# Reordering the first loads and casts of a fused dynamic convolution and squared-ReLU feed-forward kernel

## The chip, the cores and the metric

The kernel runs on one core of one Trainium2 chip. The metric is device time in microseconds (us). The profile is one execution taken by the hardware profiler. With one core busy there is no second die to compare, so the granted TensorE clock of each run (its mean as a share of full speed) is used beside its time where it matters. In this kernel TensorE does the matmuls, VectorE the softmax and the bands, ScalarE exponentials and copies, and GpSimd memsets, casts and the issue of those loads that cast on the way (casting loads).

## The reference

```python
# dynamic convolution: 7 taps per token and head, softmax over the taps
w = exp(weight_gen - max); w = w / (sum(w) + 1e-9)           # (8, 4096, 8, 7)
out = einsum('bshk,bskhg->bshg', w, x_unf)                    # x: (8, 4096, 192), causal, zero padded
# feed-forward on the 32768 tokens
h = maximum(out @ w_in, 0.0)                                  # w_in: (192, 2048)
result = (h * h) @ w_out                                      # w_out: (2048, 192), result float32
```

## The kernel before

A block is 512 tokens; there are 64. For each, softmax rows become a banded matrix ("bands", `bd`, on VectorE), small matmuls apply it to x (the convolution, `yp`), ScalarE copies the result out (`y`), and two products with w_in (`h`) and w_out (`o`) follow. Softmax weights go to DRAM (`vd`) and come back as rows (`wr`). The first block takes its rows straight from the first softmax tile (`v_first`) by small moves within the on-chip memory (row moves). The startup, cut:

```python
def cast_w_in(q, straight, crossed):
    ...
    straight(out=w_i[:, 0, c], in_=w_sa[q])
    crossed(out=w_i[RT:P, 1, c], in_=w_sa[q][0:RT])
    crossed(out=w_i[0:RT, 1, c], in_=w_sa[q][RT:P])
    straight(out=w_i[:, 2, c], in_=w_sb[q])        # last 64 rows of w_in, loaded twice
...
spin(38)                        # 38 matmuls on zeros ("warming matmuls")
band_mask()
nc.gpsimd.memset(v_first[2], 0.0)
nc.gpsimd.memset(v_big, 0.0)
...
s0.load(nc.sync)
s1.load(nc.sync)
x_load_f32(0)
load_w_in(0)
load_w_in(1)
s0.exp(0, s0.rh)
s1.exp(0, s1.rh)
x_cast(0, act)
s0.recip(0, s0.rh)
s0.scale(0, s0.rh, nc.vector)
s1.recip(0, s1.rh)
wr_load_sbuf(s0, (0, 2, 1, 3, 4), (nc.scalar, nc.gpsimd))
s0.store(nc.scalar)
cast_w_in(0, act, pool)
wr_load(1)
x_load_f32(1)
load_w_out(0)
for i in (0, 2, 1, 3, 4):
    st_band(0, (i,))
st_conv_alloc(0)
st_conv(0)
spin(4)
st_y_evac(0)
s1.scale(0, s1.rh, nc.vector)
s1.store(nc.sync)
cast_w_in(1, pool, pool)
x_cast(1, pool)
wr_load(2)
x_load(2)
load_w_out(1)
for q in range(WQ):
    cast_w_out(q, pool)
s2.load(nc.sync)
st_bands(1, 0)
st_bands(1, 1)
... # then the loop over blocks j: products of j, convolution of j+1, bands of j+2, x_load(j+3)
```

The softmax here doesn't subtract the row's maximum and nothing guards it: scores larger than these inputs give would overflow.

## Time and profile before

| | before |
|---|---|
| median of three runs | 794.05 us (792.2 to 794.29) |
| span of the profiled run | 791.0 us |
| first real product starts | 23.01 us |
| convolution of block 2 starts | 32.84 us |
| TensorE busy, 80 to 140 us | 59.96 of 60 us |

The views used are the page (busy lines, slices), the chain that ended last in order of time (start, length, what; short lines of issue and queue are left out unmarked), the timeline (start, length, engine, source line, operation, output<-input, count, and in brackets the idle time before and what ended it) and the table by stretch. The prediction shows the lines but one, the convolution of block 2 in the timeline:

```profile
32.84 0.98 PE L339 MATMUL yp<-bd,xt 128*32 128x104 f16 x72
```

### The profile page before, as it was taken

To read this page: it belongs to the slowest core of one execution; us is meant where nothing else is said; L and a number is where in the kernel's file an instruction comes from. 1 tells how busy PE (TensorE), PEld (TensorE's weight loads), DVE (VectorE), ACT (ScalarE), POOL (GpSimd) and SP (SyncE) were. 2 spreads that over 40 slices of the span, in tenths; PEclk is the share of its full clock that TensorE was granted. 3 is DMA by queue.
4 is the path that set the end of the run, shared out by engine and by line. 5 is a ranking of instruction groups with operands and counts; after the bars stand their busy time and mean duration, and the time that the engine had idled before them with its cause. 6 is when DMAs were issued, how large, how long until landed. Compare 5 with 4: busy or idle time off the path is not lost.

```text
span 791.0 us, 32666 instructions
## 1 busy us (share of the span) xinstructions
PE 773.3 (98%) x14890; PEld 679.7 (86%) x14890; DVE 586.7 (74%) x1040; ACT 605.4 (77%) x756; POOL 81.8 (10%) x98
## 2 busy tenths in 40 slices
PE   5998999999999999999999999999999999999998
PEld 2787888888888888888988888888888888888887
DVE  5888777777877768777778777877778777666653
ACT  3676877877877877877877877887787787787785
POOL 7501000010001000010001000011000010000000
PEclk9999999999999999999999999999999999999999
DMA  7862633435433543435433353333533334342111
GB/s 197 227 111 38 157 52 64 75 53 145 75 52 65 102 104 65 74 52 148 73 51 67 72 135 67 70 55 68 150 60 65 65 64 89 65 69 46 50 42 41
DMA packets 124009, 65.64 MB, mean 83 GB/s; under 512 B 84545, under 2 KB 121056, under 8 KB 123104
## 3 DMA queue, kind: packets, MB, share of 16 engines
q1 hardware_dynamic: 82032, 47.92, 21.6%
q0 software_dynamic: 40992, 15.28, 18.5%
q8 instruction: 116, 1.90, 1.1%
q10 hardware_dynamic: 848, 0.38, 0.2%
q14 instruction: 21, 0.17, 0.1%
HBM read 49.35 MB, written 29.36 MB: 100 GB/s over the span
## 4 chain that ended last, share of the span: by engine, by line
PE 93%; DMA 3%; DVE 2%; ACT 1%; issue 0%; SPq 0%; ACTq 0%; DVEq 0%
PE o L383 44%; PE h L364 43%; PE yp L339 6%; DMA wg<-in_weight_gen_dram 1%; DVE bd L290 1%; DMA wr<-v_first 1%; DMA x_st<-in_x_dram 1%; DMA vd<-v_first 0%; DVE g L400 0%; ACT t L394 0%; DVE v_big L194 0%; ACT ex L173 0%; DVE v_first L194 0%; DVE ssum L181 0%; DVE rcp L186 0%
## 5 line engine op out<-in xcount | busy, mean ns | idle before, releaser
L394 ACT ACTIVATE t<-h 128x1024 f16<-128x1024 f32 x512 | 482.8, 1031 | 9.4 <-PE h L364 8.8
L400 DVE TENSOR_TENSOR g<-t 128x1024 f16<-128x1024 f16 x512 | 346.9, 692 | 147.1 <-ACT t L394 146.9
L364 PE MATMUL h<-y,w_i 64*128 64x256 f16 x6144 | 362.5, 270 | 2.0 <-ACT y L352 1.2
L383 PE MATMUL o<-w_o,g 128*128 128x192 f16 x4096 | 360.0, 246 | 0.0
L383 PEld LDWEIGHTS <-g 128*128 128x128 f16 x4096 | 331.5, 98 | 26.8 <-DVE g L400 17.1
L364 PEld LDWEIGHTS <-w_i 64*128 64x128 f16 x6144 | 292.4, 94 | 51.0 <-issue 14.2
L290 DVE TENSOR_TENSOR bd<-wr,mask 128x1664 f16<-128x1664 f16 (+2 forms) x201 | 163.4, 844 | 11.2 <-DMA wr<-vd 6.2
L352 ACT CAST y<-yp 128x768 f16<-128x768 f32 x64 | 51.1, 798 | 122.8 <-PE yp L339 122.8
L251 POOL DMA_DIRECT2D xt<-in_x_dram x62 | 51.2, 826 | 460.4 <-PE yp L339 437.0
L405 ACT COPY o_sb<-o 128x384 f32<-128x384 f32 x127 | 62.9, 495 | 38.3 <-PE o L383 38.3
L339 PE MATMUL yp<-bd,xt 128*32 128x104 f16 (+13 forms) x4608 | 59.9, 203 | 10.6 <-DVE bd L290 10.5
L339 PEld LDWEIGHTS <-xt 128*32 128x32 f16 (+3 forms) x4608 | 51.2, 91 | 21.6 <-issue 21.5
L181 DVE TENSOR_REDUCE ssum<-ex 128x64 f32<-128x448 f32 (+6 forms) x49 | 25.9, 529 | 35.4 <-ACT ex L173 35.4
L194 DVE TENSOR_TENSOR v_big<-ex,rcp 128x112 f16<-128x112 f32 (+3 forms) x192 | 32.7, 234 | 1.6
L173 ACT ACTIVATE ex<-wg 128x448 f32<-128x448 f32 (+6 forms) x49 | 26.5, 541 | 5.0 <-DMA wg<-in_weight_gen_dram 4.9
L186 DVE RECIPROCAL rcp<-ssum 128x64 f32<-128x64 f32 (+6 forms) x49 | 23.3, 475 | 1.7
L245 POOL DMA_DIRECT2D xt<-in_x_dram x9 | 5.0, 552 | 85.2 <-PE yp L339 85.2
L442 PE MATMUL wp<-warm 128*128 128x512 f16 x42 | 12.4, 463 | 1.3 <-DVE warm L434 1.3
L241 POOL DMA_DIRECT2D xt<-in_x_dram x7 | 3.8, 541 | 77.5 <-PE yp L339 77.5
L442 PEld LDWEIGHTS <-warm 128*128 128x128 f16 x42 | 4.6, 114 | 7.9 <-issue 3.7
L194 DVE TENSOR_TENSOR v_first<-ex,rcp 128x112 f16<-128x112 f32 (+2 forms) x32 | 5.5, 242 | 0.2
L136 POOL CAST w_o<-wo_st 128x1536 f16<-128x1536 f32 x2 | 3.7, 1826 | 5.7 <-DMA wo_st<-in_moe_w_out_dram 5.7
(22 smaller groups left out, 25.5 us busy)
## 6 DMA issues: line engine op xcount, KB each, us to landing
out_dram<-o_sb SPq DMA_DIRECT2D x63, 384.0 KB, 2.8
xt<-in_x_dram POOLq DMA_DIRECT2D x46, 240.0 KB, 4.4
wg<-in_weight_gen_dram SPq DMA_DIRECT2D x6, 1064.0 KB, 6.0
wr<-vd SPq DMA_DIRECT2D x46, 80.0 KB, 3.0
vd<-v_big SPq DMA_DIRECT2D x7, 512.0 KB, 2.9
xt<-in_x_dram POOLq DMA_DIRECT2D x16, 192.0 KB, 3.9
wo_st<-in_moe_w_out_dram SPq DMA_DIRECT2D x2, 768.0 KB, 7.5
wr<-vd SPq DMA_DIRECT2D x17, 64.0 KB, 2.9
```

The lines of the kernel that those rows point to most:

```text
L173: nc.scalar.activation(out=self.ex[:, lo:hi].rearrange("p r g k e -> p (r g) k e"), in_=self.wg[:, lo:hi].rearrange("p r (g e) k -> p (r g ...
L181: nc.vector.tensor_reduce(out=ssum.rearrange("p r g e -> p (r g) e"), in_=self.ex[:, lo:hi].rearrange("p r g k e -> p (r g) e k"), axis=Ax ...
L194: eng.tensor_tensor(out=bass.AP(tensor=v.tensor, offset=v.offset + lo * H * SL + lo % SL * 2 + g * SL * 2, ap=[list(v.ap[0]), [H * SL + 2, ...
L251: eng.dma_start(out=dst[:, first:last], in_=ap)
L290: nc.vector.tensor_tensor(out=bd_t[j][:, H * lo : H * hi].rearrange("p (g m c) -> p g m c", g=shape[1], c=2 * SL), in0=wr_t[j][:, i : tile ...
L339: nc.tensor.matmul(out=yp_t[j][p0 : p0 + m, col + a : col + b], lhsT=x_t[j][:, i, 32 * q : 32 * q + m], rhs=bd[:, h // 2, h % 2, a - lo : ...
L352: nc.scalar.copy(out=y, in_=yp_t[j][:, 0 : NK * TH].rearrange("p (k c) -> p k c", k=NK))
L364: nc.tensor.matmul(out=h[:, half, jj, :], lhsT=w_i[r0 : r0 + RT, slot, fc * P : (fc + 1) * P], rhs=y_t[j][r0 : r0 + RT, k, :], start=(jj = ...
L383: nc.tensor.matmul(out=o[half][:, cc * Dm : (cc + 1) * Dm], lhsT=g_t[(j, fp)][:, half, jj, cc * P : (cc + 1) * P], rhs=w_o[:, fc, :], star ...
L394: nc.scalar.activation(out=t1, in_=h_t[(j, fp)], func=ActF.Relu)
L400: nc.vector.tensor_tensor(out=g, in0=t1, in1=t1, op=AluOp.mult)
L405: copy(out=o_sb_t[j][:, half], in_=o_t[j][half][:, 0 : 2 * Dm])
```

## The change

The change wants w_in on the chip and cast early, and keeps other first loads from delaying the first row moves (6.46 us before). In the loads, w_in comes right behind the first softmax input, and its last 64 rows are read once. ScalarE and VectorE take most casts of w_in from GpSimd. Block 1's rows too come straight from the softmax tile. The x rows of block 1 and w_out come by casting DMA from GpSimd, so their GpSimd casts go. Block 1's bands move ahead of softmax 1's sum and scale, and GpSimd's two memsets move back behind loads. The diff, cut; most of the removed lines are left out:

```diff
-        nc.sync.dma_start(out=w_sa[q], in_=moe_w_in[0:P, c])
-        for r0 in (0, RT):
-            nc.sync.dma_start(out=w_sb[q][r0 : r0 + RT], in_=moe_w_in[P:D, c])
+        nc.sync.dma_start(out=w_sa[q], in_=moe_w_in[0:P, c])
+        nc.sync.dma_start(out=w_sb[q], in_=moe_w_in[P:D, c])
...
+    def load_w_out(q, n):
+        nc.gpsimd.dma_start(out=w_o[:, q * NF // n : (q + 1) * NF // n], ...)   # f32 to f16
...
+        spin(36)
+        band_mask()
         s0.load(nc.sync)
-        s1.load(nc.sync)
-        x_load_f32(0)
         load_w_in(0)
         load_w_in(1)
+        x_load_f32(0)
         s0.exp(0, s0.rh)
         s0.recip(0, s0.rh)
         s0.scale(0, s0.rh, nc.vector)
+        cast_w_in(0, ...)                # four casts on ScalarE, one on GpSimd
+        wr_load_sbuf(0, s0, (0, 1, 2, 4, 3), (nc.sync, nc.gpsimd))
+        cast_w_in(1, "up", vec)
+        cast_w_in(1, "down", vec)
+        x_load(1)
+        s1.load(nc.sync)
+        for q in range(4):
+            load_w_out(q, 4)
+        nc.gpsimd.memset(v_first[2], 0.0)
+        x_cast(0, act)
+        wr_load_sbuf(1, s0, range(NT), (nc.sync,))
+        s0.store(nc.sync)
+        s2.load(nc.sync)
+        cast_w_in(1, "straight", act)
+        cast_w_in(1, "last", act)
         for i in (0, 2, 1, 3, 4):
             st_band(0, (i,))
         st_conv_alloc(0)
         st_conv(0)
         spin(4)
+        s1.exp(0, s1.rh)
         st_y_evac(0)
+        cast_w_in(1, "last up", act)
+        x_load(2)
+        nc.gpsimd.memset(v_big, 0.0)
+        st_bands(1, 0)
+        st_bands(1, 1)
+        s1.recip(0, s1.rh)
         s1.scale(0, s1.rh, nc.vector)
         s1.store(nc.sync)
         wr_load(2)
```

More of the change, by code (lines that the diff above doesn't have):

```diff
@@ L106, with cast_w_in @@
     WQ = 2
-    w_sa, w_sb, wo_st, x_st = {}, {}, {}, {}
+    NQ = Dff // WQ
+    w_sa, w_sb, x_st = {}, {}, {}
     def load_w_in(q):
-        n = Dff // WQ
-        c = slice(q * n, (q + 1) * n)
-        w_sa[q] = p_st.tile([P, n], f32, name="w_sa")
-        w_sb[q] = p_st.tile([P, n], f32, name="w_sb")
+        c = slice(q * NQ, (q + 1) * NQ)
+        w_sa[q] = p_st.tile([P, NQ], f32, name="w_sa")
+        w_sb[q] = p_st.tile([RT, NQ], f32, name="w_sb")
         nc.sync.dma_start(out=w_sa[q], in_=moe_w_in[0:P, c])
-        for r0 in (0, RT):
-            nc.sync.dma_start(out=w_sb[q][r0 : r0 + RT], in_=moe_w_in[P:D, c])
-    def cast_w_in(q, straight, crossed):
-        n = Dff // WQ
-        c = slice(q * n, (q + 1) * n)
-        straight(out=w_i[:, 0, c], in_=w_sa[q])
-        crossed(out=w_i[RT:P, 1, c], in_=w_sa[q][0:RT])
-        crossed(out=w_i[0:RT, 1, c], in_=w_sa[q][RT:P])
-        straight(out=w_i[:, 2, c], in_=w_sb[q])
-    def load_w_out(q):
-        n = NF // WQ
-        wo_st[q] = p_st.tile([P, n, Dm], f32, name="wo_st")
-        nc.sync.dma_start(
-            out=wo_st[q],
-            in_=moe_w_out[q * n * P : (q + 1) * n * P].rearrange("(c p) m -> p c m", p=P),
-        )
-    def cast_w_out(q, copy):
-        n = NF // WQ
-        copy(out=w_o[:, q * n : (q + 1) * n], in_=wo_st[q])
+        nc.sync.dma_start(out=w_sb[q], in_=moe_w_in[P:D, c])
+    def cast_w_in(q, op, copy):
+        c = slice(q * NQ, (q + 1) * NQ)
+        lower, upper = slice(0, RT), slice(RT, P)
+        out_p, slot, src = {
+            "straight": (slice(0, P), 0, w_sa[q]),
+            "up": (upper, 1, w_sa[q][lower]),
+            "down": (lower, 1, w_sa[q][upper]),
+            "last": (lower, 2, w_sb[q]),
+            "last up": (upper, 2, w_sb[q]),
+        }[op]
+        copy(out=w_i[out_p, slot, c], in_=src)
+    def load_w_out(q, n):
+        nc.gpsimd.dma_start(
+            out=w_o[:, q * NF // n : (q + 1) * NF // n],
+            in_=moe_w_out[q * Dff // n : (q + 1) * Dff // n].rearrange(
+                "(c p) m -> p c m", p=P
+            ),
+        )
     class Softmax:
@@ L268, in wr_load, with wr_load_sbuf @@
         block_load(j, wr, vd_t[j // NBB], H * SL, nc.sync)
-    def wr_load_sbuf(s, order, engines):
-        wr_t[0] = p_wr.tile([P, NT, HP, SL * 2], f16, name="wr")
+    def wr_load_sbuf(j, s, order, engines):
+        wr_t[j] = p_wr.tile([P, NT, HP, SL * 2], f16, name="wr")
         for n, i in enumerate(order):
-            t0 = max(starts[i], 0)
+            t0 = max(j * TB + tile_start(j, i), 0)
             engines[n % len(engines)].dma_start(
-                out=wr_t[0][:, i].rearrange("p g c -> p (g c)"),
+                out=wr_t[j][:, i].rearrange("p g c -> p (g c)"),
                 in_=s.v[t0 // s.r : (t0 + P) // s.r, HALO : HALO + s.r].rearrange(
@@ L444, in spin @@
                 )
-        spin(38)
-        band_mask()
-        nc.gpsimd.memset(v_first[2], 0.0)
-        nc.gpsimd.memset(v_big, 0.0)
-        vec, act, pool = nc.vector.tensor_copy, nc.scalar.copy, nc.gpsimd.tensor_copy
         def softmax(s, lo, hi):
@@ L455, in softmax @@
             s.scale(lo, hi, nc.vector)
+        vec, act, pool = nc.vector.tensor_copy, nc.scalar.copy, nc.gpsimd.tensor_copy
         s0, s1, s2 = parts
+        spin(36)
+        band_mask()
         s0.load(nc.sync)
-        s1.load(nc.sync)
-        x_load_f32(0)
         load_w_in(0)
         load_w_in(1)
+        x_load_f32(0)
         s0.exp(0, s0.rh)
-        s1.exp(0, s1.rh)
-        x_cast(0, act)
         s0.recip(0, s0.rh)
         s0.scale(0, s0.rh, nc.vector)
-        s1.recip(0, s1.rh)
-        wr_load_sbuf(s0, (0, 2, 1, 3, 4), (nc.scalar, nc.gpsimd))
-        s0.store(nc.scalar)
-        cast_w_in(0, act, pool)
-        wr_load(1)
-        x_load_f32(1)
-        load_w_out(0)
+        cast_w_in(0, "straight", act)
+        cast_w_in(0, "up", act)
+        cast_w_in(0, "down", pool)
+        cast_w_in(0, "last", act)
+        cast_w_in(0, "last up", act)
+        wr_load_sbuf(0, s0, (0, 1, 2, 4, 3), (nc.sync, nc.gpsimd))
[12 more added lines that the diff above has]
+        cast_w_in(1, "last", act)
         for i in (0, 2, 1, 3, 4):
@@ L479 @@
         spin(4)
+        s1.exp(0, s1.rh)
         st_y_evac(0)
+        cast_w_in(1, "last up", act)
[4 more added lines that the diff above has]
+        s1.recip(0, s1.rh)
         s1.scale(0, s1.rh, nc.vector)
         s1.store(nc.sync)
-        cast_w_in(1, pool, pool)
-        x_cast(1, pool)
         wr_load(2)
-        x_load(2)
-        load_w_out(1)
-        for q in range(WQ):
-            cast_w_out(q, pool)
-        s2.load(nc.sync)
-        st_bands(1, 0)
-        st_bands(1, 1)
         plan = {}
```

## The prediction

Cut from the text below, each cut marked, are statements of how the hardware behaves that no trace or run shows, and what rests on them. The first product's start is the author's estimate; 19.4 is 17.0 plus the 2.4 us of before. The forecast's sum came to 3.2 us (1.8 at block 2's convolution and 1.4 at the third softmax load), 4.3 in its better case, and 4.0 was taken. Rival B's point was that the casting loads of w_out and x run just when the second row moves, softmax 1's store and block 2's rows are wanted.

> **What bounds the kernel now.** I read the busy lines and the forty slices first. TensorE is busy in nearly every slice at full clock; only the first and, slightly, the last are not.
>
> ```profile
> PE 773.3 (98%) x14890; PEld 679.7 (86%) x14890; DVE 586.7 (74%) x1040; ACT 605.4 (77%) x756; POOL 81.8 (10%) x98
> ...
> PE   5998999999999999999999999999999999999998
> ...
> PEclk9999999999999999999999999999999999999999
> ```
>
> So the steady part is a TensorE bound. In the timeline one block of 512 tokens takes 12.0 and then 11.8 us (convolution matmuls at 76.22, 88.22 and 100.02), and the table by stretch has 59.96 us busy of 60 between 80 and 140 us. Of the parts of a block in the chain (convolution 0.83, first product 2 x 2.73, second 2 x 2.75) I make 11.79 us, times 64 blocks 754.6 us. The span is 791.0, so all that is not a full TensorE is 36 us: 23.0 before the first real product, some 4 at the tail, the rest scattered before 72 us. The diff touches only code before the block loop, so it can win from the first 23 us and from stalls that follow from them, nothing else.
>
> Next I read the chain that ended last, in order of time, for the first 80 us (columns: start, length, what):
>
> ```profile
> 2.19 5.71 DMA x_st<-in_x_dram
> ...
> 7.98 0.58 ACT xt L263
> 8.56 6.46 DMA wr<-v_first
> ...
> 15.12 5.48 DVE bd L290 x5
> 20.60 1.38 DVE v_first L194 x8
> ...
> 22.00 3.20 DMA vd<-v_first
> ...
> 26.19 8.62 DMA wg<-in_weight_gen_dram
> ...
> 35.57 0.78 ACT y L352
> ```
>
> Three things are to be seen. The five small row moves (16 KB each) from the first softmax tile take 6.46 us; the five band products that they feed take 5.48 us; later the load for the third softmax part takes 8.62 us and holds up ScalarE, so that TensorE waits for y at 36.4. The timeline of TensorE has the effect:
>
> ```profile
> 16.16 0.27 PE L339 MATMUL yp<-bd,xt 128*32 128x104 f16 x2 [4.32 <-DVE bd L290]
> 17.50 0.62 PE L339 MATMUL yp<-bd,xt 128*32 128x56 f16 x22 [1.07 <-DVE bd L290]
> 18.85 0.27 PE L339 MATMUL yp<-bd,xt 128*32 128x104 f16 x2 [0.72 <-DVE bd L290]
> 20.19 1.19 PE L339 MATMUL yp<-bd,xt 128*32 128x104 f16 x46 [1.07 <-DVE bd L290]
> 21.31 1.77 PE L442 MATMUL wp<-warm 128*128 128x512 f16 x4
> 23.01 2.79 PE L364 MATMUL h<-y,w_i 64*128 64x256 f16 x48
> ```
>
> [...] 6.2 to 6.5 us for the moves while w_in streams, 1.7 us for a 16 KB load when the engines are idle (at 16.26). [...] bands finish some 1.33 us apart while GpSimd casts w_in, against the row by form beyond 60 us:
>
> ```profile
> L290 DVE TENSOR_TENSOR bd<-wr,mask 128x832 f16<-128x832 f16 x14 | 7.7, 586 | 1.4 <-DMA wr<-vd 1.2
> ```
>
> [...] Here the idle window 12.59 to 16.00 is followed by 0.50 until 22.8. [...] all casting x loads here stand in GpSimd's queue.
>
> **The change, part by part.**
>
> *Loads.* Before, the queue holds s0 (401 KB), s1 (401), x (491) and w_in with its last 64 rows loaded twice (2,097 KB). Now it holds s0, w_in with those rows loaded once (1,573) and x: 2,465 KB. The rate was about 250 GB/s while w_in ran (mean of 7 to 15 us: 253). S0 is through at 3.4 us, w_in 6.3 us later at 9.7, x after 1.4 at its own 350 GB/s: 11.1. The slowest engine landed 1.8 us after this average before (second w_sa at 14.55, where the sum of bytes says 12.75). I put x at 12.8.
>
> *Row moves.* Softmax 0 is unchanged and ends at 8.53. Three of its five moves now stand in the same queue behind x, the other two in GpSimd's. Their few pieces follow x, beside casting loads of the other queue: 14.0 for the last needed ones, against 15.1. So the moves gain about 1 us only.
>
> *Bands 0.* GpSimd no longer casts at that time (one of its six w_in casts stays, at about 7 to 8 us; ScalarE and VectorE take the others). 5 x 0.586 is 2.9, with gaps 3.0 instead of 5.48: 14.0 to 17.0. The two VectorE casts of w_in lie in its wait before 14.
>
> *First product.* ScalarE does x cast, two w_in casts and the s1 exponential between 12.8 and 17 (0.99 + 2 x 1.04 + 0.96 = 4.0), just in time for y. In before, the first product came 2.4 us after the last band (20.6 to 23.0) at half clock. [...] So it starts at 19.0 to 19.4, some 3.8 us earlier. [...]
>
> *What comes after on VectorE.* Now bands 1 go before softmax 1's sum and scale. Bands 1: 2 x 1.017 + 0.55 = 2.6. Reduce and reciprocal, formerly hidden in the wait for row moves, now lie on the path: 0.97 + 0.85 = 1.8; scale 1.44. From 17.0, with 0.5 of wait for the second row moves, this ends at 23.4; the same scale ended at 21.97 before. Its store (2.8) and the load of block 2's rows (2.8) put bands 2 at 29.0 and the convolution of block 2, after two products of 1.02, at 31.0. Before it was 32.84. TensorE itself could be there at 28.9, so about 2 us of the early start are given back as a wait.
>
> *Third softmax load.* It is issued near 14 instead of 26.19 and lands long before use. The waits of 1.2 and 0.3 us at 35 to 37 us go: 1.4 us gained, rounded.
>
> *w_out.* 1,573 KB are read by four casting loads in place of two plain loads and two GpSimd casts (1.5 + 2.2 us, off the path). Four casting x loads moved 838 KB of f16 from 38 to 43 us, 168 KB per us; w_out is 786 KB of f16, so 4.7 us, and the two x loads 491 KB, 2.9. They end by about 24 to 25, w_out's first half near 18, before the second product needs it at about 26. Hidden.
>
> *Sum.* 1.8 at block 2's convolution plus 1.4 at the softmax load is 3.2 us; if the row moves land at 13.2 and the store chain keeps pace, 4.3. I take 4.0. The stall at 58.9 to 62.5 stays: it runs from a TensorE product through the next softmax and bands, in unchanged order. 794.05 - 4.0 = 790.0 us.
>
> **Rivals.**
>
> A. *The whole early start survives.* If stores and row loads take 2.1 to 2.2 us each, as some did on quiet engines, and bands 0 start at 13, block 2's convolution is at 28.5 and the gain is 4.3 + 1.4, with a warm clock some 7: 787. For it: the code in the loop has no bound but TensorE. Against it: the VectorE chain is serial, and its own sum is worked out above.
>
> B. *Contention eats it.* [...] For it: a row load issued at 26.82 behind large loads took 8.2 us. Against it: that one stood behind them in its own queue. 2 to 3 us more on the path leaves a gain of 1: 793.
>
> C. *Bands or convolution wait for x or s1.* ScalarE casts in program order and x now lands after w_in; a late x or s1 holds y up behind it. I see up to 1.5 us: 791.5.
>
> D. *All hidden.* The chain shares (93% TensorE) suggest it, but before 23 us nothing is hidden: every microsecond there is in the span. Unlikely.
>
> **Range and chances.** A and B bound it: 787 and 793, widened by the spread of before (792.2 to 794.29). 786.5 to 793.5. A gain of over 2% would need 15.9 us of the 36 lost, more than the first product can move; a loss of over 2% would need a new wait in the loop. I give 0.01, 0.98, 0.01.
>
> **What would show it.** In the changed trace: bands of 0.59 us instead of 1.33; row moves landing at 13 to 14.5; first product at 18.5 to 19.5; scale of softmax 1 ending at 23 to 24; a TensorE wait before block 2's convolution named by its bands or rows; no wait for the third softmax load; the stall near 59 us present but earlier; a block pitch of 11.8 us unchanged. Wrong would be: a first product later than 21, a wait for w_out, slow bands although GpSimd doesn't cast[...], or slower casting loads than 168 KB per us.

## The result, and the profile after

A ratio here is the mean time of one kernel's fast runs over that of the other kernel's fast runs of the same rounds, so it is not quite the ratio of the medians quoted. The changed kernel took 792.84 us (median of 4; 791.82 to 792.96) against 794.17 (median of 4), ratio 0.9983, 95% interval 0.9961 to 1.0005. That is about 1.35 us faster where 4 were predicted, and the interval includes no gain. The time lies inside the predicted range; the gain is about a third of the predicted one.

The slices of the page of the changed kernel (TensorE and its clock; a slice is 19.7 us):

```profile
PE   7889999999999999999999999999999999999997
...
PEclk8998999999999999999999999999999999999999
```

TensorE's first slice is fuller than before (7 instead of 5). But the clock now has marks below 9 in the first and fourth slice, so a part of that busy time is at a lower clock: by the table by stretch it was 0.50 from 15 to 21 us, and from 60.4 to 63.8. The timeline of TensorE:

```profile
16.11 1.18 PE L338 MATMUL yp<-bd,xt 128*32 128x104 f16 x46 [0.23 <-DVE bd L289]
...
19.04 3.96 PE L363 MATMUL h<-y,w_i 64*128 64x256 f16 x48
...
31.55 0.22 PE L338 MATMUL yp<-bd,xt 128*32 128x104 f16 x2 [1.72 <-DVE bd L289]
32.39 0.91 PE L338 MATMUL yp<-bd,xt 128*32 128x56 f16 x70 [0.62 <-DVE bd L289]
```

The first product comes 4.0 us earlier than before, as wanted. The main part of block 2's convolution comes only 0.45 us earlier. The chain that ended last names what lies between:

```profile
14.12 5.50 DMA wr<-v_first
...
22.01 1.47 DVE v_first L193 x8
23.49 4.01 DMA vd<-v_first
...
27.55 2.80 DMA wr<-vd
30.38 1.97 DVE bd L289 x2
```

Block 1's last row move lands at 19.6. The bands, sum and scale follow (to 23.47), then a store of 128 KB in 4.01 us (3.20 before) and block 2's rows. TensorE finished the second product at 29.8 and waits for this.

What stands beside that path is in the table of DMA queues for 14 to 30 us (packets, MB, and their time as a share of 16 engines' time), first before, then changed. The queue of GpSimd's casting loads went from 13.4% to 102.9%:

```profile
q0 software_dynamic: 633, 0.24, 13.4%
```

```profile
q0 software_dynamic: 5194, 1.93, 102.9%
```

When w_out landed is in the same table for 14.5 to 15 us, in its list of issues (KB each, us from issue to landing):

```profile
w_o<-in_moe_w_out_dram POOLq DMA_DIRECT2D x1, 192.0 KB, 8.4
```

This is the last of the four w_out loads. Issued at 14.0, it landed at 22.4, before the store began; beside the store were the x loads of blocks 3 to 5, which landed at 25.9, 27.1 and 29.1. The two kinds of loads thus meet different parts of the path. The third softmax load (616 KB, from 15.64, 7.9 us) was under way too; no run moved it.

I set the milestones side by side, from timelines and chains, with a second profile of the same changed kernel from another session ("again", run `a_again` below):

| us | before | changed | again |
|---|---|---|---|
| bands 0 start | 15.12 | 13.95 | 14.11 |
| five bands 0 take | 5.48 | 2.57 | 2.57 |
| first product starts | 23.01 | 19.04 | 19.20 |
| block 1's last row move lands | - | 19.62 | 20.70 |
| softmax 1 scaled | 21.97 | 23.47 | 24.55 |
| its store takes | 3.20 | 4.01 | 4.84 |
| bands 2 start | 29.16 | 30.38 | 31.84 |
| convolution of block 2, main part | 32.84 | 32.39 | 33.86 |
| second product of block 0, second half | 38.09 | 35.97 | 38.68 |
| block 4's main convolution + the first product after it (block 3's) | 0.91 + 4.46 | 1.46 + 4.78 | 0.92 + 4.46 |
| convolution of block 5 | 76.22 | 74.98 | 76.83 |
| span | 791.0 | 789.8 | 791.6 |

The whole difference between the kernels is settled by 75 us: 1.2 us at block 5's convolution, 1.2 at the end. Two of the expectations (`a_spin`, `b_spin`) call the product after block 4's convolution block 4's; by the code of the loop it is block 3's.

### The profile page after: what moved, and what is told of

It is laid out like the page before. It is cut to its first block, busy times and chain, and to the rows that moved or that the text cites. A ratio compares the mean times of both kernels' runs of the same rounds, so it can differ in the third digit from the quotient of the medians.

```text
span 789.8 us, 32661 instructions
## 1 busy us (share of the span) xinstructions
PE 774.0 (98%) x14888; PEld 680.1 (86%) x14888; DVE 584.0 (74%) x1042; ACT 610.7 (77%) x761; POOL 73.6 (9%) x96
## 3 DMA queue, kind: packets, MB, share of 16 engines
q0 software_dynamic: 43776, 16.31, 19.5%
## 4 chain that ended last, share of the span: by engine, by line
PE 94%; DMA 3%; DVE 2%; SPq 0%; ACT 0%; issue 0%; DVEq 0%
PE o L382 44%; PE h L363 44%; PE yp L338 7%; DMA x_st<-in_x_dram 1%; DMA wr<-v_first 1%; DVE bd L289 1%; DMA vd<-v_first 1%; DMA wr<-vd 0%; DVE g L399 0%; DVE ssum L180 0%; DVE rcp L185 0%; DVE v_big L193 0%; DVE v_first L193 0%; ACT ex L172 0%; SPq L115 0%
## 5 line engine op out<-in xcount | busy, mean ns | idle before, releaser
L289 DVE TENSOR_TENSOR bd<-wr,mask 128x1664 f16<-128x1664 f16 (+2 forms) x201 | 160.8, 832 | 15.4 <-DMA wr<-vd 12.6
L250 POOL DMA_DIRECT2D xt<-in_x_dram x63 | 52.2, 830 | 472.3 <-PE yp L338 448.4
L338 PE MATMUL yp<-bd,xt 128*32 128x104 f16 (+12 forms) x4608 | 60.4, 204 | 10.0 <-DVE bd L289 6.1
L180 DVE TENSOR_REDUCE ssum<-ex 128x64 f32<-128x448 f32 (+6 forms) x49 | 25.9, 529 | 32.9 <-ACT ex L172 32.9
L244 POOL DMA_DIRECT2D xt<-in_x_dram x10 | 5.7, 569 | 86.9 <-PE yp L338 86.9
L240 POOL DMA_DIRECT2D xt<-in_x_dram x7 | 3.8, 543 | 78.0 <-PE yp L338 78.0
L127 ACT CAST w_i<-w_sa 128x1024 f16<-128x1024 f32 (+1 forms) x3 | 3.1, 1043 | 1.4 <-DMA w_sa<-in_moe_w_in_dram 1.4
```

Source lines behind the costliest of these rows:

```text
L180: nc.vector.tensor_reduce(out=ssum.rearrange("p r g e -> p (r g) e"), in_=self.ex[:, lo:hi].rearrange("p r g k e -> p (r g) e k"), axis=Ax ...
L250: eng.dma_start(out=dst[:, first:last], in_=ap)
L289: nc.vector.tensor_tensor(out=bd_t[j][:, H * lo : H * hi].rearrange("p (g m c) -> p g m c", g=shape[1], c=2 * SL), in0=wr_t[j][:, i : tile ...
L338: nc.tensor.matmul(out=yp_t[j][p0 : p0 + m, col + a : col + b], lhsT=x_t[j][:, i, 32 * q : 32 * q + m], rhs=bd[:, h // 2, h % 2, a - lo : ...
```

## The experiments

**Theory S/W (contention).** The early start of TensorE is real, but the path to block 2 is set by another chain: block 1's row moves, softmax 1, its store, block 2's rows. The casting loads of w_out and of later x, now running at exactly that time, lengthen it. **Theory C (clock).** Part of the gain goes where the clock falls to half (0.50 from 16 to 22.8 us before). **Theory L (GpSimd work beside VectorE's).** Such work makes VectorE slower, and this is why the bands were slow before: five took 5.48 us beside GpSimd's casts, while one of that form took 586 ns beyond 60 us. **Rivals:** the gain is 4 us and the first comparison was noise; w_out is hidden; the order of block 1's bands and softmax 1 is what costs.

Each kernel was timed in five rounds beside the kernel before, in three sessions of four kernels. The 11 runs of before in each had medians of 793.31 us (`a_again`, `a_xbufs2`, `a_s1first`, `a_spin`), 793.8 (`a_nowout`, `a_wouthw`, `a_gate`, `a_best`) and 792.26 (`a_best2`, `a_best3`, `b_spin`, `b_actcast`).

### The changed kernel again

> The changed kernel itself, once more, for a tighter ratio. Theory S (the gain of the start is lost on the path softmax 1 scale, store, row load, bands 2, and a rest to the half clock near 60 us): the ratio stays near 0.9983, that is 1 to 2 us faster, and the trace again has the first product about 4 us early, the convolution of block 2 under 1 us early. Rival N (the first comparison was noise, the real gain is the predicted 4 us): ratio near 0.995.

Measured: 793.51 us, ratio 1.0001 (0.9981 to 1.002). Theory S's 1 to 2 us did not come, and the rival's 4 us still less. The table shows how: the first product came as early as the first time, but the row moves landed at 20.70, the store took 4.84 us, and block 2's convolution came after the time of before. Its chain:

```profile
24.57 4.84 DMA vd<-v_first
...
29.46 2.36 DMA wr<-vd
31.84 1.98 DVE bd L289 x2
```

TensorE waited 3.7 us there, the clock fell (mean 0.54 from 33.5 to 37 us), and the first product after the convolution, block 1's, took 3.50 us instead of 2.79. The two estimates of what the change is worth are thus 1.4 us and nothing.

### Two x buffers

```diff
-    p_x = ctx.enter_context(tc.tile_pool(name="p_x", bufs=4))
+    p_x = ctx.enter_context(tc.tile_pool(name="p_x", bufs=2))
```

> Two x buffers instead of four, so that the casting loads of blocks 2, 3 and 4 can no longer start before the convolutions of blocks 0, 1 and 2 have read theirs (about 17, 24 and 33 us instead of 16, 20 and 21). Theory S with contention (the store of softmax 1 takes 4.0 us because early x loads fill the DMA engines): the store lands in about 3.0 us, bands 2 start near 29.3 instead of 30.38, and the kernel gains about 1 us on the changed one. Rival R (the store takes 4 us in itself, or w_out holds it up): the store still takes 3.8 us or more and nothing is gained.

Measured: 790.84 us, ratio 0.997 (0.9948 to 0.9992). The chain:

```profile
13.89 6.61 DMA wr<-v_first
20.60 1.49 DVE bd L289 x2
...
25.38 2.60 DMA vd<-v_first
...
28.04 2.10 DMA wr<-vd
```

The store and the row load fell to 2.60 and 2.10 us, from 4.01 and 2.80 in the first profile of the changed kernel and 4.84 and 2.36 in the second. So the early x loads do lengthen them. Before, GpSimd came to block 3's x load only at 35.3 us, behind its casts and a wait of 5.66 us for w_out's second half, and in the changed kernel it does so at 19.5. Bands 2 started at 30.16 and not at 29.3 as expected, because block 1's row moves took 6.61 us: these loads are not what delays those. The gain on `a_again` in the same session, 2.5 us, is more than the 1 us expected. Some of it may be the clock: in this profile the product after block 4's convolution took 2.79 us, in that of `a_again` 4.46, and the clocks of the six runs were 0.991 to 0.996 against 0.989 to 0.993.

### Softmax 1 first

```diff
-        st_bands(1, 0)
-        st_bands(1, 1)
         s1.recip(0, s1.rh)
         s1.scale(0, s1.rh, nc.vector)
         s1.store(nc.sync)
         wr_load(2)
+        st_bands(1, 0)
+        st_bands(1, 1)
```

> Undoes one move of the change: softmax 1's sum, scale and store go before the bands of block 1 again. Theory S: the scale ends near 20.7 instead of 23.5, the store even at 4.5 us lands by 25.2, bands 2 start near 28.3, and the convolution of block 2 follows the second product with next to no wait; about 2 us faster than the changed kernel. Rival B1 (block 1's bands then come too late for its convolution): a wait of over 1 us before the convolution of block 1, and no gain.

Measured: 791.76 us, ratio 0.9981 (0.9957 to 1.0005): no clear gain. The profiled run is the slowest of the six (795.1; the others 789.24 to 793.92). In it the scale ended at 19.9, even earlier than expected, but:

```profile
19.94 5.46 DMA vd<-v_first
25.45 5.57 DMA wr<-vd
```

Store and rows took 11.0 us together, where 7.6 were allowed for, with casting x loads issued at 16.76, from 19.98 to 22.2 and at 23.34. Bands 2 started at 31.05 instead of 28.3. Rival B1's wait before block 1's convolution was only 0.61 us. In this profile the order alone did not help while the casting loads ran beside the store and the rows.

### Idle matmuls before block 4's convolution

```diff
                     st_conv_alloc(j + 1)
+                    if j == 3:
+                        for _ in range(12):
+                            nc.tensor.matmul(out=yp_t[4][:, 0:TB], lhsT=warm[:, 0:P],
+                                             rhs=warm, start=True, stop=True)
                     st_conv(j + 1)
```

> The changed kernel with 12 idle matmuls (2.6 us) put into the wait before the convolution of block 4 near 57 us. Theory C (0.9 us of the early start is lost there because the half clock falls on more of the following matmuls than in the kernel before): the convolution and first product of block 4 take 0.9 and 2.8 us instead of 1.5 and 4.8, and the kernel is about 2.5 us faster than the changed one. Rival: the idle matmuls delay the convolution or the clock falls all the same, and nothing is gained.

Measured: 792.02 us, ratio 0.9985 (0.9966 to 1.0005). The timeline of TensorE shows that they do what they should:

```profile
59.30 2.75 PE L531 MATMUL yp<-warm 128*128 128x512 f16 x12
...
63.03 0.91 PE L338 MATMUL yp<-bd,xt 128*32 128x56 f16 x70 [0.71 <-DVE bd L289]
63.88 2.79 PE L363 MATMUL h<-y,w_i 64*128 64x256 f16 x48
```

Against the same kernel without them (1.0001 in the same session) the difference is about 1.3 us, under the 2.5 expected and inside the intervals. In the same profile the row moves took 7.67 us and block 2's convolution began at 33.43.

### The same in the kernel before

> The kernel before with the same 12 idle matmuls as in a_spin before block 4's convolution. Its trace showed 4.46 us instead of 2.79 for the first product of block 4, so it should gain 1 to 1.7 us. If it gains as much as the changed kernel did with them (a_spin against a_again and the first result: 0.2 to 1.3 us), the clock does not favour either kernel and theory C explains the scatter from run to run, not the missing gain.

Measured: 791.24 us, ratio 0.9986 (0.9972 to 1.0). The two gains are alike (about 1.1 us here, 1.3 there). With block 4's convolution and the product after it at 0.91 and 2.79 us in both profiles (without the idle matmuls 0.91 and 4.46 before, 1.46 and 4.78 or 0.92 and 4.46 changed), their ratios to the kernel before are the same, 0.9985 and 0.9986. So there is no sign that the clock there favours one of them; without the idle matmuls the product's time differs from profile to profile (2.79 us in `a_xbufs2`). Of the 33 runs of the kernel before in these three sessions, the four with a granted clock of 0.995 took 791.06 to 791.61 us, the three with 0.989 took 794.63 to 796.07; whether the clock sets the time or both follow from the same waits, these figures don't tell. That spread is larger than the effect under study.

### Without w_out (wrong result)

```diff
+        nc.gpsimd.memset(w_o, 0.01)      # right after band_mask()
...
-        for q in range(4):
-            load_w_out(q, 4)
```

> The changed kernel without the w_out loads: w_o is filled by one memset at the start, so the result is wrong on purpose. Theory W (the four casting w_out loads share the DMA engines with the second row moves and cost the path 1 to 4 us there): the last of the second row moves lands by about 17 instead of 19.6 to 22, bands 1 follow bands 0 with under 0.5 us of waits, softmax 1's scale ends near 22.4, and the convolution of block 2 starts 1.5 us or more earlier than in both profiles of the changed kernel. Rival X (early x loads alone are the cause): the moves still land at 19.5 or later.

Measured: 791.15 us, ratio 0.9967 (0.9952 to 0.9981); the result is wrong, as it must be. The chain:

```profile
12.14 3.93 DMA wr<-v_first
...
21.89 2.22 DMA vd<-v_first
...
24.16 3.23 DMA wr<-vd
27.41 1.97 DVE bd L289 x2
29.43 0.91 PE yp L338 x56
```

The last awaited row move took 3.93 us and landed at 16.07, the store 2.22, and the convolution of block 2 began at 29.43, 3.0 and 4.4 us earlier than in the two profiles of the changed kernel (of this, 1.4 and 1.5 us were there already at the first product, at 17.66). Theory W holds for the row moves: the w_out loads keep no product waiting, and yet cost the path: with them the last awaited row move took 5.50 and 6.22 us. The short store is not theirs alone: w_out had landed before the store in the changed kernel too, and without the four issues GpSimd sent the x loads of blocks 3 and 4 2.8 us earlier (from 16.75), so that less of them was left beside it.

### w_out alone undone

```diff
-        for q in range(4):
-            load_w_out(q, 4)
...
         s2.load(nc.sync)
+        load_w_out_plain(0)              # f32 loads on the plain queue
+        load_w_out_plain(1)
...
         nc.gpsimd.memset(v_big, 0.0)
+        for q in range(2):               # cast by GpSimd as before
+            pool(out=w_o[:, q * NF // 2 : (q + 1) * NF // 2], in_=wo_st[q])
```

> The changed kernel with w_out alone undone: two plain loads behind the third softmax load, two casts on GpSimd. Theory W: the second row moves land by about 17.5 as without w_out; the price is that GpSimd's casts near 20 to 25 us may slow VectorE and softmax 1's store stands behind 1.6 MB in its own queue (lands 3 to 4 us after issue). On balance 0.5 to 1.5 us faster than the changed kernel. Rival: queue order costs what the casting loads cost, no gain.

Measured: 794.54 us, ratio 1.0003 (0.9962 to 1.0045), in two groups: 788.68, 790.4 and 791.27, and 797.82, 797.9 and 799.91. The profile is of a run of the first group. There the row moves landed at 18.4, but the store, behind w_out in its own queue, took 4.70 us, and the second product of block 0 waited 2.6 us for GpSimd's cast of w_out. So here large plain loads ahead in the queue cost the store about as much as casting loads (4.01 and 4.84). What makes the slow group slow no trace shows; this run settles nothing about the balance of the two ways.

### Half of w_out and the later x loads held back

```diff
-        for q in range(4):
+        for q in range(2):
             load_w_out(q, 4)
...
         wr_load(2)
+        gate = const.tile([P, 2], f16, name="gate")
+        nc.gpsimd.tensor_copy(out=gate, in_=wr_t[2][:, 0, 0, 0:2])   # GpSimd waits for block 2's rows
+        for q in range(2, 4):
+            load_w_out(q, 4)
```

> The changed kernel with half of w_out and all x loads from block 3 on held back in GpSimd's queue until block 2's rows have landed (a copy of two numbers of them makes GpSimd wait). Theory W plus S: second row moves land near 18, the store takes 2.6 us and the row load 2.1 us as with two x buffers, the convolution of block 2 starts near 29 to 30, and no second product waits for w_out; 2 to 3 us faster than the changed kernel. Rival: the held-back half of w_out comes too late and the second product of block 0 waits for it near 34.

Measured: 791.39 us, ratio 0.9966 (0.9951 to 0.9981), 2.7 us faster than before. The expected 2 to 3 us were against the changed kernel, which was not timed in the same rounds; against its two ratios, 0.9983 and 1.0001, it is 1.3 or 2.8. The profiled run went another way: block 2's convolution began at 34.11 without a wait for it. The timeline of VectorE, and then that of GpSimd, show a new cost:

```profile
11.52 7.65 DVE L127 CAST w_i<-w_sa 64x1024 f16<-64x1024 f32 x2 [2.55 <-DMA w_sa<-in_moe_w_in_dram]
19.20 1.09 DVE L289 TENSOR_TENSOR bd<-wr,mask 128x832 f16<-128x832 f16 x2
```

```profile
13.28 1.66 POOL L473 MEMSET v_first<- 128x1792 f16 x1
...
15.65 2.97 POOL L489 MEMSET v_big<- 128x2816 f16 x1
```

Two casts that took 1.48 us in the changed kernel took 7.65, beside GpSimd's memsets, which had moved forward because two loads ahead of them were gone. They held up the bands of block 0 to 19.2. The first of the two was slow (2.9 us) though it began 1.8 us before the first memset's record, beside load issues; spans on GpSimd are rough.

### The three together

`a_best` is the held-back kernel with softmax 1 first and the 12 idle matmuls.

> The three together: w_out's second half and the later x loads held back, softmax 1's scale before the bands of block 1, and 12 idle matmuls in the wait before block 4's convolution. If the three causes add up: scale ends near 20, store 2.6, rows 2.1, so bands 2 could start near 25 and TensorE reaches the convolution of block 2 without a wait near 29; the clock stays full at block 4. 4 to 6 us faster than the kernel before, about 788. If one of them only moves a wait: 790 or more.

Measured: 788.8 us, ratio 0.9938 (0.9919 to 0.9958), about 4.9 us faster than before (0.0062 of 793.8). The scale ended at 22.3, later than expected, as the two casts took 5.40 us in this profile too. Block 2's convolution began at 31.52, without a wait. No run takes one of the three parts out again, so their shares are not known; the idle matmuls alone gave the kernel before about 1.1 us.

### The memsets moved behind

```diff
-        nc.gpsimd.memset(v_first[2], 0.0)     # both before the gate
-        nc.gpsimd.memset(v_big, 0.0)
...
         for q in range(2, 4):
             load_w_out(q, 4)
+        nc.gpsimd.memset(v_first[2], 0.0)
+        nc.gpsimd.memset(v_big, 0.0)
```

> As a_best, with GpSimd's two memsets (1.6 and 2.9 us) moved behind the held-back w_out loads. Theory L ([...] in a_gate and a_best the second of the two casts ran into the memsets and the two took 7.7 and 5.4 us instead of 1.5, which held up the bands of block 0): the two casts take 1.5 us, bands 0 start at 13 to 14 instead of 16.4 to 19.2, the first product near 18.5, and the kernel is 2 to 3 us faster than a_best, near 786. Rival: the casts were late for their data, and nothing changes.

Measured: 786.96 us (786.62 to 789.09), ratio 0.9931 (0.9916 to 0.9946): 5.5 us faster than before (0.0069 of 792.26). The intervals of this and `a_best` overlap, so a gain of 2 us over it is not shown. What is shown is what became of the two casts with the memsets moved behind, in the timeline of VectorE:

```profile
11.91 1.84 DVE L127 CAST w_i<-w_sa 64x1024 f16<-64x1024 f32 x2 [3.61 <-DMA w_sa<-in_moe_w_in_dram]
14.73 2.57 DVE L289 TENSOR_TENSOR bd<-wr,mask 128x832 f16<-128x832 f16 x5 [0.99 <-DMA wr<-v_first]
```

The casts are back at 1.84 us, from 7.65 in `a_gate` and 5.40 in `a_best`, and the first product came at 19.77 instead of 21.53. In this profile, the slowest of the six runs, the second product then waited 1.7 us for the held-back half of w_out. The rows for the gate had landed, but the copy of two numbers itself took 5.47 us; in `a_best` and `a_best3` it took 0.73 and 0.95. All three ran beside VectorE work, so why this one was long stays open:

```profile
25.70 5.47 POOL L495 COPY gate<-wr 128x2 f16<-128x2 f16 x1 [10.81 <-DMA wr<-vd]
```

### More warming matmuls

```diff
-        spin(36)
+        spin(44)
```

> As a_best2 with 44 warming matmuls instead of 36 at the start, which closes 1.7 us of the wait before the first convolution. Theory C: the clock stays full through block 0, its 46 last convolution matmuls take 0.6 to 0.9 us and not 1.2, the four idle ones 0.9 and not 1.9, so the first product comes 1 us earlier than in a_best2; since everything up to the convolution of block 2 is then set by TensorE, the total falls by up to 1 us. Rival: softmax 1's store and block 2's rows are the limit and the total stays.

Measured: 787.33 us (786.4 to 788.73), ratio 0.9935 (0.992 to 0.995): the same as `a_best2`. The first product came at 18.61, but it took 3.54 us instead of 2.79, and the four idle matmuls before it took 1.89 us, as in the changed kernel at a clock of 0.50 (1.04 in `a_wouthw`), although the wait before the first convolution was only 1.04 us. The total stayed, as the rival said, but not for its reason: block 2's convolution began at 29.07 without a wait for its bands. The early start was partly lost to these slower matmuls. The profiled run is the fastest of the six; of the others there is no trace.

### One part of the change alone, in the kernel before

```diff
         cast_w_in(0, act, pool)
+        cast_w_in(1, act, act)
...
-        cast_w_in(1, pool, pool)
```

> The kernel before with one part of the change alone: the second half of w_in is cast by ScalarE, which waits there, and not by GpSimd. Theory L (bands of block 0 take 1.33 us each because GpSimd's casts hold VectorE off): the five bands take 2.6 to 3.0 us instead of 5.48, the first product comes 2 to 3 us earlier (20 to 21 instead of 23.0), and the kernel is 1.5 to 2.5 us faster than before. Rival: the bands stay slow because their rows land one after the other, and the total stays.

Measured: 792.24 us, ratio 0.9996 (0.9978 to 1.0014). The timeline of VectorE:

```profile
15.13 2.57 DVE L290 TENSOR_TENSOR bd<-wr,mask 128x832 f16<-128x832 f16 x5 [5.09 <-DMA wr<-v_first]
```

Moving this half's four casts from GpSimd to ScalarE, and nothing else, halves the bands from 5.48 to 2.57 us, and the first product comes at 19.83 instead of 23.01. Theory L holds for the bands. The expected 1.5 to 2.5 us of total did not show: the profiled run was 788.7 us long against 791.0, but that run is the fastest of six, which range from 790.45 to 793.9. Its store took 5.03 us, behind plain loads of its own queue, so an early start runs into loads here too. Most of the early start that the change buys is this one part.

## Why the prediction was right or wrong

**Right.** The bound, the place of the possible gain and the order of the chain were right: the 4 us at the first product came, and the give-back before block 2's convolution was foreseen, at about 2 us; it was 3.5. Bands 0 at 14.0 (measured 13.95 and 14.11), the first product at 19.0 to 19.4 (19.04 and 19.20) and softmax 1 scaled at 23.4 (23.47; again 24.55) came as forecast. The bands sped up because GpSimd no longer cast beside them, as `b_actcast` shows (5.48 to 2.57 us). That TensorE would wait before block 2's convolution, and that the block pitch would stay, held too.

**Wrong: "Its store (2.8) and the load of block 2's rows (2.8) put bands 2 at 29.0".** The store took 4.01 and 4.84 us (2.60 with the later x loads held back, `a_xbufs2`), and bands 2 started at 30.38 and 31.84. This step failed. The term of the store, 1.2 to 2.0 us too small, takes most of the 1.8 us that the sum had at block 2's convolution: measured were 0.45 us gained and 1.0 us lost. "With 0.5 of wait for the second row moves" was the second mis-sized term: the row moves took 5.5 to 7.7 us in profiles of the changed kernel and of that kernel with the idle matmuls, and the waits between bands were 1.05 us in the first and 1.88 in the second. In the first profile bands 0, at 0.51 us each instead of 0.59, happened to make up for it, so softmax 1 was scaled on time; in the second it was 1.1 us late.

**Wrong: "Hidden", of w_out.** The step asked whether a product waits for w_out. None does. But the loads run beside moves that are on the path, and without them the row moves landed 3.6 and 4.6 us and block 2's convolution came 3.0 and 4.4 us earlier (`a_nowout`). A sign of being wrong that the prediction named was there: the 786 KB of w_out took from 11.8 to 22.4 us, 74 KB per us and not 168. The step also counted only two x loads. GpSimd, freed of its casts, issued those of blocks 3 to 5 between 19.5 and 24.2 us, into the store. This is rival B of the prediction, which was given 793 us and set aside with the argument that the slow row load seen before had stood behind large loads in its own queue. It had, but casting loads in another queue cost the path too: with w_out's the last awaited row move took 5.50 and 6.22 us, without them 3.93; with the later x loads the store took 4.01 and 4.84, with these held back 2.60.

**Partly wrong: the third softmax load, 1.4 us.** The waits went. In the first profile the lead grew by 1.7 us from block 2's convolution to the second product. In the second profile only 0.4 of it was left, as the clock was low after the wait before block 2 (mean 0.54 from 33.5 to 37 us).

**Mis-sized or left out: the clock.** The first product took 3.96 us in the first profile, where the clock was 0.50 from 15 to 21 us, and 3.00 in the second, against 2.79. That was hidden in the wait before block 2. Not foreseen was the rest: after the wait near 57 us block 4's convolution and the next product took 0.9 us longer than before in the first profile and the same in the second. `a_spin` and `b_spin` give no sign that this favours a kernel; but single profiles differ by such amounts.

**Wrong: "I take 4.0".** The sum was 3.2 us; the rest leaned on its better case of 4.3, which asked that the row moves land at 13.2 and the store keep pace. Bands 0 started at 13.95, and the store took 4.01.

What stays open: how much the changed kernel really gains. The two sessions give 0.9983 and 1.0001 with intervals that overlap; anything from nothing to about 1.4 us fits. How much of the long row moves is due to w_out and how much to the third softmax load and the store of softmax 0, which ran beside them too, is not separated. The slow group of `a_wouthw` is not explained either.

## What to carry to other kernels

A load that nobody waits for was not free here while small transfers on the critical path ran beside it: the last awaited row move took 3.93 us without the w_out loads, 5.50 and 6.22 with them. It can be held back behind an event of that path (here a two-element copy on the issuing engine, which itself can be held up: 5.47 us in one profile). With that, softmax 1 first, the memsets moved and the idle matmuls, the reordering was worth 5.5 us instead of at most about 1.4; about 1.1 of it the idle matmuls gave the kernel before as well. When work is taken off an engine that also issues DMAs, ask what it will issue earlier, and into what (here the x loads of blocks 3 to 5, the first at 19.5 us instead of 35.3, into softmax 1's store). Where the effect is below the scatter from run to run, compare milestones inside the traces, from more than one profile.

## Sizes that the runs show

- Small transfers on the critical path, with and without casting loads of GpSimd beside them: a 128 KB store took 2.60 us with the later x loads held back, 4.01 and 4.84 with them, and 5.46 in `a_s1first`, issued at 19.94 with x loads behind it from 19.98 to 22.2; an 80 KB row load took 5.57 there and 2.10 with two x buffers; the last awaited 16 KB row move took 3.93 without the w_out loads, 5.50 and 6.22 with them.
- VectorE beside GpSimd: five bands took 2.57 us partly beside a memset (14.77 to 16.41) in the changed kernel, and 5.48 beside casts in the kernel before. Two VectorE casts took 7.65 us beside memsets and load issues (`a_gate`), and 1.39 to 1.84 us without the memsets. A GpSimd copy of two numbers per partition, beside VectorE work, took 5.47 us in one profile, 0.73 and 0.95 in two.
- The clock: 33 runs of one kernel lay between 791.06 and 796.07 us, with granted clocks between 0.995 and 0.989, while the changes under study were 1 to 5 us. In the kernel before, TensorE was busy for 0.89, 0.23 and 1.54 us of the three stretches of 2 us from 58 to 64, and had not waited over 2.73 us at a time since 24 us; the clock was 1.00, 1.00 and 0.95 in them, and 0.50 from 64 to 66.
